# Weight pairs of the second mixture: which of them are made ready at which turn

## The chip, the cores and the metric

The kernel runs on one core of a Trainium2 chip. A time is the device time of one execution in microseconds; where several runs are given it is their median. The engines are named as in the profile: PE is TensorE (PEld its weight loads), DVE is VectorE, ACT is ScalarE, POOL is GpSimd and SP the engine whose queue issues the DMAs.

## What is computed

Three parts follow one another: an attention that keeps the 32 largest scores of a row, a mixture of 8 experts in which each of 2304 tokens goes to one expert, and a second mixture in which every token goes through every expert. Only the second mixture is changed. Cut to that:

```python
def _moe2_ref(x, w_gate, w1, w2):            # x: 2304 x 512, w1: 8 x 512 x 1024, w2: 8 x 1024 x 512
    logits = x @ w_gate
    logits = logits - logits.max()
    P = np.exp(logits)
    for _ in range(8):
        P /= P.sum(1, keepdims=True) + 1e-09
        P /= P.sum(0, keepdims=True) + 1e-09
        P *= N / E
    out = np.zeros((N, D))
    for e in range(E):
        h = np.maximum(x @ w1[e], 0.0)
        out += P[:, e:e + 1] * (h @ w2[e])
    return out
```

## The kernel before

**Split numbers.** Every matrix product is made of three passes: a float is split into a high part (`...h`, a rounded copy that ScalarE makes, line 117) and a low part (`...l`, what the copy left out, a subtraction, line 118), and `mm3` adds high x high, high x low and low x high (lines 848 to 850, in another order of operands for the second product). So weights have to be split before they are used.

**Steps.** The second mixture goes through 8 experts (`e`), for each through 9 blocks of 256 tokens (`blk`), for each through 4 quarters of the hidden layer (`i`): 288 steps, counted by `s`; 36 of them are an expert. In step s TensorE first makes the hidden quarter in one PSUM buffer `ph`, 24 matmuls (`first`, line 1089), and then takes the quarter of the step before through w2 into the banks, 21 matmuls (`second`, line 1183). There is one `ph`: the next step's matmuls may start only when ScalarE (`z`, line 1104) and VectorE (four operations on `z`, line 1103) have read it. ScalarE then makes `hh` in two parts (lines 1105 and 1111) and VectorE `hl` in two (lines 1112 and 1113), which the next step's `second` reads. The 21 matmuls stand for 24: `second` works by Strassen's scheme with seven products of quarters, so w2 needs sums of its quarters.

**Sum pieces.** After a block's fourth quarter `gather_up` (line 1125) lists the operations that turn the seven products into the output: one copy on ScalarE and, on VectorE, sums that read a bank (line 1142) and, from expert 1 on, puts into `acc` (line 1148, all operands in SBUF); 12 in all (8 or 10 in expert 0, two stores more in expert 7). `settle(k)` issues the next k of them.

**Weight pairs.** An expert's w1 and w2 are each four pairs of 128 rows of the hidden layer; pair i is used in quarter i. To make a w1 pair is one step: two ScalarE copies and two GpSimd subtractions (`w1h`, `w1l`). To make a w2 pair has two halves (`strassen`, line 125). Half a: `w2h` on ScalarE and `w2l` on VectorE, twice each (256 and 512 columns), and then four sums of the raw tiles on GpSimd (`raw`, line 129). Half b, which reads what these leave: `w2h`, `w2l`, `w3h`, `w3l`. A pair may be made when its buffer is free: 6 w1 pairs and 5 w2 pairs are kept, so that pairs 2 and 3 of the next expert's w1, and 1 to 3 of its w2, can be made only when the last block (s % 36 from 32 on) has used the present expert's. The pair that becomes free after these belongs to the expert beyond the next. A loaded pair waits in `queue`; `loads` (line 905) keeps one w1 pair and two w2 pairs in it, and the DMAs stand on SP's queue in that order.

**What sets the order.** The loop over s writes out, for each step, the operations of `first`, `second`, the sum pieces (`settle`, line 1252) and then the weight work (`work`, line 1253); each engine takes its own in this order. The work and the pieces written at the end of turn s run on ScalarE and VectorE between the `hl` of step s and the `z` of step s + 1, so in step s + 1. `work(2)` takes up to two items of the queue a turn, begun ones first, then by number, as soon as their buffers are free. In turns 1 to 18 the gate's normalisation (`sink`: `sk`, `ck`, lines 1071 to 1085) stands there too.

Of the kernel before, what the change touches and what calls it, by code (L numbers as in the profile page):

```python
# [22 lines left out]
N = B * S  # L23
# [44 lines left out]
def fused_kernel(ctx, tc, qT, kT, vv, wg1, w1a, w2a, wg2, w1b, w2b, out):  # L68
# [37 lines left out]
    def w_load(pool, src, tag, bufs):  # L106
        raw = pool.tile([128, 2, 256], F32, name="raw", tag=tag, bufs=bufs)
        nc.sync.dma_start(raw.rearrange("p a b -> p (a b)"), src)
        return raw

    def w_tiles(name, pool=None, bufs=NFC // 2):
        pool, k = pool or wpool, {"w1": 4, "w2": 5, "w3": 2}[name]
        return [pool.tile([128, k, 256], F32R, name=name + x, tag=name + x, bufs=bufs) for x in "hl"]

    def split(t, s, raw, eng):

        return [lambda: A.activation(t[0][:, s], raw, AF.Copy),  # L117
                lambda: eng.tensor_tensor(out=t[1][:, s], in0=raw, in1=t[0][:, s], op=OP.subtract)]  # L118
# [6 lines left out]
    def strassen(t, t2, b1, b2):  # L125


        b11, b12, b21, b22 = b1[:, 0], b1[:, 1], b2[:, 0], b2[:, 1]
        seq = [lambda o=o, x=x, y=y, op=op: G.tensor_tensor(out=o, in0=x, in1=y, op=op)  # L129
                for o, x, y, op in ((b11, b12, b11, OP.subtract), (b12, b22, b12, OP.subtract),  # L130
                                    (b22, b11, b22, OP.subtract), (b21, b21, b22, OP.add))]
        return [split(t, slice(0, 1), b1[:, 0:1], V) + split(t, slice(1, 3), b2, V), seq,
                split(t, slice(3, 5), b1, V) + split(t2, slice(0, 2), b2, V)]
# [698 lines left out]
    def ids_out():  # L832

        for k in range(3):
            nc.sync.dma_start(id_dram.rearrange("(e k p) o -> p k e o", k=3, p=96)[:, k], g96[:96, k, :, None])

    def ids_in():
        nc.sync.dma_start(slot_ids, id_dram.rearrange("(t p) o -> p (t o)", p=128))
# [17 lines left out]
    gone = {"w1": 0, "w2": 0}  # L856
    loaded = {"w1": NFC // 2, "w2": NFC // 2}
    queue = []
    turns = [0]

    more = {}

    def places(n, g):
        return NFC // 2 + (EXTRA[n] if g >= 36 else 0)

    def make(n, g, raws):
        at = (more[n], EXTRA[n]) if g >= 36 and (g - 36) % places(n, g) < EXTRA[n] else ()
        W[n, g] = t = w_tiles(n, *at)
        if n == "w2" and g >= 32:
            W["w3", g] = w_tiles("w3", *(at or (w3,)))  # L870
            return strassen(t, W["w3", g], *raws)
        eng = (V, G) if g < 32 else (G, G)
        return [[x for f in range(2) for x in split(t, slice(2 * f, 2 * f + 2), raws[f], eng[f])]]

    def load(n):
        g = loaded[n]
        loaded[n] += 1
        e, i = divmod(g % 32, 4)
        src = ((w1a, w1b) if n == "w1" else (w2a, w2b))[g // 32]
        raws = [w_load(rw, src[e, 2 * i + f], n, 2 if n == "w1" else 4) for f in range(2)]  # L880
        queue.append([n, g, raws, None, 0])

    def work(budget):

        turns[0] += 1
        after = []
        for item in sorted(queue, key=lambda q: (-q[4], q[1], q[0])):
            n, g, raws, stages, second_turn = item
            if g >= gone[n] + places(n, g) or budget < 1 or g >= 36 and not more:
                continue  # L890
            budget -= 1
            if stages is None:
                item[3] = stages = make(n, g, raws)
            for f in stages.pop(0):
                f()
            if stages and second_turn == 0:
                item[4] = 1
                after += stages.pop(0)
            if not stages:
                queue.remove(item)  # L900
        for f in after:
            f()
        loads()

    def loads():
        for n, room in (("w1", 1), ("w2", 2)):
            while loaded[n] < 8 * NFC and sum(q[0] == n for q in queue) < room:
                load(n)

    def need(n, g):  # L910
        for item in list(queue):
            if item[:2] == [n, g]:
                for stage in item[3] or make(n, g, item[2]):
                    for f in stage:
                        f()
                queue.remove(item)
        return W[n, g]
# [5 lines left out]
    def banks(k):  # L923
        return bank[k].rearrange("p a b -> p (a b)")

    def half_bank(k):
        return bank[k // 2][:, k % 2]
# [16 lines left out]
    def turn(xg, d, parts, pt=None, ks=(0, 1, 2)):  # L944
        if not parts:
            parts += [xg_p.tile([128, NDC, CAP], F32R, name=n, bufs=2) for n in ("xgh", "xgl")]
        if pt is None:
            pt = ps.tile([128, 2, 256], F32, name="ph").rearrange("p a b -> p (a b)")
        for k in ks:
            PE.transpose(pt[:, k * 96:(k + 1) * 96], xg[k][:96, d * 128:(d + 1) * 128], identf[:96, :96])  # L950

        def after():
            A.activation(parts[0][:, d], pt[:, :CAP], AF.Copy)
            V.tensor_tensor(out=parts[1][:, d], in0=pt[:, :CAP], in1=parts[0][:, d], op=OP.subtract)
        return after
# [24 lines left out]
    def load_x(blk):  # L980
        t = x_tiles(xs, 2)
        for k in range(2):
            nc.sync.dma_start(all_of(t[k]).bitcast(F32), xp_dram[blk][k])
        return [(t[0][:, d], t[1][:, d]) for d in range(NDC)]
# [17 lines left out]
    for k in range(3):  # L1002
        for i in range(GBUSY[k]):
            PE.matmul(banks(4), onesb, onesb[:, None, :].to_broadcast([128, 4, 128]), start=True, stop=True)
        after = [turn(xg, d, nxt, banks(d), (k,)) for d in range(NDC)]
# [3 lines left out]
    for e in range(E):  # L1009
        x, nxt = nxt, []  # L1010
        for f in range(NFC):
            w1 = need("w1", 4 * e + f // 2)
# [74 lines left out]
    sink = [(logits_end, max_a), (max_t, max_b)] + [(lambda pm: None, rows), (sums_t, columns)] * 8  # L1087
# [95 lines left out]
    def second(e, blk, i, h):  # L1183
        w2 = need("w2", 32 + 4 * e + i)
        for k in range(7):
            q = (0, 5, 1, 3, 6, 4, 2)[k]
            w = [x[:, q] for x in w2] if q < 5 else [x[:, q - 5] for x in W["w3", 32 + 4 * e + i]]
            mm3(half_bank(half(e, blk, k)), (h[0][:, k], h[1][:, k]), w,
                i == 0 and k in (0, 1, 3, 5), i == NFC // 2 - 1, skip_group_check=True)

    nb = N // 256
    pend, sums = None, []

    def settle(k):
        for _, g in sums[:k]:
            g()
        del sums[:k]

    steps = E * nb * 4
    for s in range(steps + 1):  # L1200
        eb, i = divmod(s, 4)
        e, blk = divmod(eb, nb)

        pm = half_bank(13 if (s - 1) // 4 % 2 == 0 else 5)
        if s < steps:
            if i == 0:
                x = xa.pop(0)
            h = first(need("w1", 32 + 4 * e + i), x)
            if i == 3 and eb + 2 < E * nb:
                xa.append(load_x((blk + 2) % nb))  # L1210
            if blk == nb - 1:
                gone["w1"] += 1
        if s == 40:
            ids_out()
        if s == 80:
            ids_in()
        if s and sink:
            sink[0][0](pm)
        if pend is None:
            second1(*last1)  # L1220
            part1.close()
            sx = turned.enter_context(tc.tile_pool(name="sx", bufs=1))
        else:
            while sums and sums[0][0] < pend[0] * nb + pend[1] - 1:
                settle(1)
            second(*pend)
            if pend[1] == nb - 1:
                gone["w2"] += 1
            if pend[2] == 3:
                b = pend[0] * nb + pend[1]  # L1230
                sums += [(b, g) for g in gather_up(*pend[:2])]
        if s == steps:
            settle(len(sums))
            break
        if s and sink:
            sink.pop(0)[1](pm)
            if not sink:
                sums += scales
        pend = (e, blk, i, h)
        if s < nb - halved:  # L1240

            xt = x_tiles(sx, 2)
            for d in range(NDC):
                split_x(xt, halved + s, d)
        if s == 3:
            turned.close()
            ac = late["ac"] = ctx.enter_context(tc.tile_pool(name="ac", bufs=1))
            late["acc"] = ac.tile([128, NT, D], F32, name="acc")
        if s == 6:
            more["w1"] = ctx.enter_context(tc.tile_pool(name="w1x", bufs=1))  # L1250
            more["w2"] = ctx.enter_context(tc.tile_pool(name="w2x", bufs=1))
        settle(5 if len(sums) > 12 or sink else 3)
        work(2)


# [42 lines left out]
```

## Time and profile before

| what | value |
|---|---|
| median of 3 runs | 2373.21 us (2372.59 to 2375.51) |
| the profiled execution | 2370.71 us, of which the span of its instructions 2368.9 |
| granted TensorE clock, mean over the span | 0.983 of full speed (1.00 in the second mixture) |
| the second mixture | from about 775 us to the end, 67% of the span |
| PE busy in the span | 2274.4 us (96%), 19592 matmuls |
| DVE, ACT, POOL busy | 1682.4 (71%), 1184.6 (50%), 709.9 us (30%) |

A matmul here takes 0.28 us from start to end, and the next one starts some 0.12 us after it: they overlap, so TensorE's share of busy time says little. What counts is how many matmuls run in a stretch, and where one starts late. The profile gives for each line how often an engine stood idle before it and what ended that wait; the views of single stretches show what stood in the way.

### The profile page before, as it was taken

The numbers are of one execution on the slowest core, as the hardware profiler recorded it, in microseconds if no ns is written. First come the engines' busy times: TensorE is split into PE (matmuls) and PEld (weight loads), VectorE is DVE, ScalarE is ACT, GpSimd is POOL, SyncE is SP. The second block draws the span as 40 slices with busy tenths as digits, with TensorE's granted clock in tenths as the row PEclk, the third lists the DMA queues.
The fourth block names the chain that finished last, engine by engine and source line by source line (L and its number), as shares of the span: only waits on it lengthen the run. The fifth ranks groups of instructions, "written<-read, shape, count | busy, mean of one in ns | idle before, by whom it ended". The sixth has DMA issues, their size and how long they took to land.

```text
span 2368.9 us, 49352 instructions
## 1 busy us (share of the span) xinstructions
PE 2274.4 (96%) x19592; PEld 2157.8 (91%) x19592; DVE 1682.4 (71%) x4320; ACT 1184.6 (50%) x2549; POOL 709.9 (30%) x792
## 2 busy tenths in 40 slices
PE   9999999949999899999999999999999999999998
PEld 6888888728999899999999999999999999999998
DVE  8999999873444676766776686686677668667665
ACT  8999999714555433533443343353344334334332
POOL 6888888604445200400210030040021003002011
PEclk9999999869999999999999999999999999999999
DMA  2102010015665411311221131131122113112111
GB/s 80 56 28 66 26 57 15 21 68 162 203 203 182 166 55 55 118 44 55 90 79 47 63 116 37 54 119 43 54 90 79 48 63 114 40 54 72 70 69 50
DMA packets 78048, 184.29 MB, mean 78 GB/s; under 512 B 13424, under 2 KB 13680, under 8 KB 77808
## 3 DMA queue, kind: packets, MB, share of 16 engines
q1 hardware_dynamic: 74832, 171.61, 21.8%
q0 software_dynamic: 2976, 9.44, 1.1%
q8 instruction: 156, 2.56, 0.4%
q14 instruction: 84, 0.69, 0.1%
HBM read 162.13 MB, written 18.88 MB: 76 GB/s over the span
## 4 chain that ended last, share of the span: by engine, by line
issue 41%; PE 25%; POOL 5%; DVE 3%; DMA 2%; ACT 1%; POOLq 0%; SPq 0%; DVEq 0%; ACTq 0%
PE bank L848 5%; PE bank L850 5%; PE bank L849 5%; POOL raw L129 4%; PE ph L848 3%; PE ph L849 3%; PE ph L850 3%; POOL w1l L118 1%; DMA raw<-in_w1b_dram 1%; DVE z L1103 1%; DVE w2l L118 1%; POOL out_dram L1169 0%; PE bank L961 0%; DVE hl L1113 0%; ACT w1h L117 0%
## 5 line engine op out<-in xcount | busy, mean ns | idle before, releaser
L848 PE MATMUL ph<-xh,w1h 128*128 128x256 f32 x2304 | 649.5, 282 | 40.1 <-DVE z L1103 26.6
L849 PE MATMUL ph<-xl,w1h 128*128 128x256 f32 x2304 | 646.1, 280 | 1.0 <-DMA xl<-xpl 1.0
L850 PE MATMUL ph<-xh,w1l 128*128 128x256 f32 x2304 | 645.9, 280 | 0.0
L1103 DVE SCALAR_TENSOR_TENSOR z<-ph,z 128x128 f32<-128x128 f32 x1152 | 308.2, 288 | 425.0 <-ACT z L1104 405.3
L1104 ACT ACTIVATE z<-ph 128x512 f32<-128x512 f32 x288 | 171.6, 596 | 691.3 <-PE ph L850 690.9
L118 POOL TENSOR_TENSOR w1l<-raw,w1h 128x512 fp32r<-128x512 f32 x92 | 122.6, 1345 | 1213.4 <-ACT w1h L117 1200.5
L848 PEld LDWEIGHTS ph<-xh,w1h 128*128 128x128 f32 x2304 | 434.2, 188 | 47.4 <-issue 45.4
L849 PEld LDWEIGHTS ph<-xl,w1h 128*128 128x128 f32 x2304 | 433.8, 188 | 1.3 <-DMA xl<-xpl 1.3
L850 PEld LDWEIGHTS ph<-xh,w1l 128*128 128x128 f32 x2304 | 433.8, 188 | 0.0
L848 PE MATMUL bank<-w2h,hh 128*128 128x256 f32 x1440 | 405.2, 281 | 0.0
L850 PE MATMUL bank<-w2h,hl 128*128 128x256 f32 x1440 | 404.1, 281 | 0.0
L849 PE MATMUL bank<-w2l,hh 128*128 128x256 f32 x1440 | 403.4, 280 | 0.0
L1111 ACT ACTIVATE hh<-z 128x512 fp32r<-128x512 f32 x288 | 182.2, 633 | 220.0 <-DVE z L1103 220.0
L850 PEld LDWEIGHTS bank<-w2h,hl 128*128 128x128 f32 x1440 | 271.7, 189 | 0.0
L849 PEld LDWEIGHTS bank<-w2l,hh 128*128 128x128 f32 x1440 | 271.5, 189 | 0.0
L848 PEld LDWEIGHTS bank<-w2h,hh 128*128 128x128 f32 x1440 | 271.1, 188 | 0.0
L1113 DVE TENSOR_TENSOR hl<-z,hh 128x512 fp32r<-128x512 f32 x288 | 214.9, 746 | 58.6 <-ACT hh L1111 58.6
L271 POOL TENSOR_TENSOR W<-W,sg 128x288 f32<-128x288 f32 x288 | 208.2, 733 | 69.4 <-ACT sg L266 68.9
L256 DVE MAX8 upper<-W 128x8 f32<-128x288 f32 x432 | 183.2, 448 | 5.7 <-POOL W L271 4.3
L338 PEld LDWEIGHTS pO<-vt,aT 128*128 128x128 f32 x1280 | 159.6, 193 | 28.2 <-issue 26.3
L1112 DVE TENSOR_TENSOR hl<-z,hh 128x384 fp32r<-128x384 f32 x288 | 170.9, 593 | 0.0
L295 POOL TENSOR_TENSOR dbuf<-S,upper 128x576 f32<-128x576 f32 x144 | 165.2, 1147 | 0.0
(234 smaller groups left out, 4804.5 us busy)
## 6 DMA issues: line engine op xcount, KB each, us to landing
xh<-xph SPq DMA_DIRECT2D x72, 512.0 KB, 3.3
xl<-xpl SPq DMA_DIRECT2D x72, 512.0 KB, 4.2
raw<-in_w1a_dram SPq DMA_DIRECT2D x64, 256.0 KB, 3.1
raw<-in_w2a_dram SPq DMA_DIRECT2D x64, 256.0 KB, 2.9
raw<-in_w2b_dram SPq DMA_DIRECT2D x64, 256.0 KB, 2.8
raw<-in_w1b_dram SPq DMA_DIRECT2D x64, 256.0 KB, 2.7
vt<-in_vv_dram SPq DMA_DIRECT2D x16, 325.0 KB, 3.8
kt<-in_kT_dram SPq DMA_DIRECT2D x16, 288.0 KB, 3.5
```

Source lines behind the costliest of these rows:

```text
L118: lambda: eng.tensor_tensor(out=t[1][:, s], in0=raw, in1=t[0][:, s], op=OP.subtract)]
L256: V.max(out=upper[:, ST[n]["at"], 8 * k:8 * k + 8], in_=ST[n]["W"])
L271: G.tensor_tensor(out=d["W"], in0=d["W"], in1=d["sg"], op=OP.mult)
L295: G.tensor_tensor(out=flat(d["D"])[:, :S], in0=flat(d["S"]), in1=upper[:, d["at"], 0:1].to_broadcast([128, S]), op=OP.subtract)
L848: PE.matmul(dst, a[0], b[0], start=start, stop=False, **kw)
L849: PE.matmul(dst, a[0], b[1], start=False, stop=False, **kw)
L850: PE.matmul(dst, a[1], b[0], start=False, stop=stop, **kw)
L1103: V.scalar_tensor_tensor(out, q[:, k], 0.0, y, op0=OP.max, op1=op)
L1104: A.activation(z[:, :4], q, AF.Relu)
L1111: A.activation(hh[:, 3:], z[:, 4:], AF.Copy)
L1112: V.tensor_tensor(out=hl[:, :3], in0=z[:, 1:4], in1=hh[:, :3], op=OP.subtract)
L1113: V.tensor_tensor(out=hl[:, 3:], in0=z[:, 4:], in1=hh[:, 3:], op=OP.subtract)
```

## The change

The second mixture's loop no longer calls `work(2)` but `chosen(s)` and `work2`. `due` gives a pair the turn in which it is first used. `chosen` looks at the queue in the order of these turns and takes at most one w2 half and one w1 pair a turn: a pair that is due within 12 turns, or, on every second turn of the quiet middle of an expert (s % 36 from 10 to 31), one pair that is due later. A w1 pair due in more than 2 turns stands back when a w2 pair is begun. The pieces of the sums are issued 2 a turn beside a w2 half, else 4 (5 while the normalisation lasts); before it was 3 (5 as long as more than 12 wait or the normalisation lasts). The first mixture still calls `work(1)`.

```diff
--- before.py
+++ after.py
@@ -859,6 +859,7 @@
     turns = [0]
 
     more = {}
+    nb = N // 256
 
     def places(n, g):
         return NFC // 2 + (EXTRA[n] if g >= 36 else 0)
@@ -906,6 +907,43 @@
         for n, room in (("w1", 1), ("w2", 2)):
             while loaded[n] < 8 * NFC and sum(q[0] == n for q in queue) < room:
                 load(n)
+
+    def due(n, g):
+
+        e, i = divmod(g - 32, 4)
+        return 4 * nb * e + i + (n == "w2")
+
+    def chosen(s):
+
+
+        quiet = 10 <= s % (4 * nb) < 4 * nb - 4
+        todo = {}
+        for item in sorted(queue, key=lambda q: due(*q[:2])):
+            n, g = item[:2]
+            if g >= gone[n] + places(n, g) or g >= 36 and not more:
+                continue
+            if due(n, g) - s <= 12 or quiet and s % 2 == 0 and not todo:
+                todo.setdefault(n, item)
+        if "w1" in todo and "w2" in todo and todo["w2"][4] == 0 and due(*todo["w1"][:2]) - s > 2:
+            del todo["w1"]
+        return [todo[n] for n in ("w2", "w1") if n in todo]
+
+    def work2(items):
+        after = []
+        for item in items:
+            n, g, raws, stages, begun = item
+            if stages is None:
+                item[3] = stages = make(n, g, raws)
+            for f in stages.pop(0):
+                f()
+            if stages and not begun:
+                item[4] = 1
+                after += stages.pop(0)
+            if not stages:
+                queue.remove(item)
+        for f in after:
+            f()
+        loads()
 
     def need(n, g):
         for item in list(queue):
@@ -1188,7 +1226,6 @@
             mm3(half_bank(half(e, blk, k)), (h[0][:, k], h[1][:, k]), w,
                 i == 0 and k in (0, 1, 3, 5), i == NFC // 2 - 1, skip_group_check=True)
 
-    nb = N // 256
     pend, sums = None, []
 
     def settle(k):
@@ -1249,8 +1286,9 @@
         if s == 6:
             more["w1"] = ctx.enter_context(tc.tile_pool(name="w1x", bufs=1))
             more["w2"] = ctx.enter_context(tc.tile_pool(name="w2x", bufs=1))
-        settle(5 if len(sums) > 12 or sink else 3)
-        work(2)
+        items = chosen(s)
+        settle(5 if sink else 2 if items and items[0][0] == "w2" else 4)
+        work2(items)
 
 
 # ---- launch: one core; the host lays the arrays out, nothing more ----
```

The change writes the same operations in another order. ScalarE's order at the turn from expert 1 to 2, before: the work of turn s = 69 (w2 half a and a w1 pair), one step, and the work of s = 70 (half b of that pair, half a of the next). `z<-ph` is the first operation of a step.

```order
L117 ACTIVATE w2h<-raw 128x256
L117 ACTIVATE w2h<-raw 128x512
L117 ACTIVATE w1h<-raw 128x512 x2
L1104 ACTIVATE z<-ph 128x512
L1105 ACTIVATE hh<-z 128x384
L1111 ACTIVATE hh<-z 128x512
L117 ACTIVATE w2h<-raw 128x512
L117 ACTIVATE w3h<-raw 128x512
L117 ACTIVATE w2h<-raw 128x256
```

And in the changed kernel, the same two turns (its lines 1142, 1143 and 1149 are 1104, 1105 and 1111 of before):

```order
L117 ACTIVATE w2h<-raw 128x256
L117 ACTIVATE w2h<-raw 128x512
L1142 ACTIVATE z<-ph 128x512
L1143 ACTIVATE hh<-z 128x384
L1149 ACTIVATE hh<-z 128x512
L117 ACTIVATE w2h<-raw 128x512
L117 ACTIVATE w3h<-raw 128x512
L117 ACTIVATE w1h<-raw 128x512 x2
L1142 ACTIVATE z<-ph 128x512
```

The w1 pair has moved from beside half a to beside half b, and the next pair's half a is gone from the second turn; it stands in the turn after it.

VectorE's order over the same two turns, before: the last put of a turn's three pieces, half a, the four `z` and two `hl` of step 70, three pieces, half b, and half a of the next pair.

```order
L1148 SCALAR_TENSOR_TENSOR acc<-u_27020,L_19455,acc 128x256
L118 TENSOR_TENSOR w2l<-raw,w2h 128x256
L118 TENSOR_TENSOR w2l<-raw,w2h 128x512
L1103 SCALAR_TENSOR_TENSOR z<-ph,z 128x128 x4
L1112 TENSOR_TENSOR hl<-z,hh 128x384
L1113 TENSOR_TENSOR hl<-z,hh 128x512
L1142 TENSOR_TENSOR c_27018<-c_27018,bank_19470 128x256
L1148 SCALAR_TENSOR_TENSOR acc<-c_27018,L_19455,acc 128x256
L1142 TENSOR_TENSOR u_27177<-u_27022,bank_19471 128x256
L118 TENSOR_TENSOR w2l<-raw,w2h 128x512
L118 TENSOR_TENSOR w3l<-raw,w3h 128x512
L118 TENSOR_TENSOR w2l<-raw,w2h 128x256
```

In the changed kernel (1186, 1141, 1150, 1151 and 1180 are 1148, 1103, 1112, 1113 and 1142 of before):

```order
L1186 SCALAR_TENSOR_TENSOR acc<-u_27020,L_19455,acc 128x256
L118 TENSOR_TENSOR w2l<-raw,w2h 128x256
L118 TENSOR_TENSOR w2l<-raw,w2h 128x512
L1141 SCALAR_TENSOR_TENSOR z<-ph,z 128x128 x4
L1150 TENSOR_TENSOR hl<-z,hh 128x384
L1151 TENSOR_TENSOR hl<-z,hh 128x512
L1180 TENSOR_TENSOR c_27018<-c_27018,bank_19470 128x256
L1186 SCALAR_TENSOR_TENSOR acc<-c_27018,L_19455,acc 128x256
L118 TENSOR_TENSOR w2l<-raw,w2h 128x512
L118 TENSOR_TENSOR w3l<-raw,w3h 128x512
L1141 SCALAR_TENSOR_TENSOR z<-ph,z 128x128 x4
```

The second turn has lost one piece and the two `w2l` of the next pair's half a; step 71's `z` follows `w3l` at once.

## Rows read from the trace of the kernel before

**Rows 1.** Waits of TensorE, 779 to 2350 us: total, times, longest.
```profile
PE ph L848 <- DVE z L1103: 26.6, 29, 1.5
```
**Rows 2.** Busy time by stretch: length, then PE, PEld, DVE, ACT, POOL (x instructions), clock, DMA.
```profile
1010.00:1157.00 147.00, 147.00 (x1245) 147.00 (x1245) 91.17 (x242) 50.15 (x89) 0.00 (x0) 1.00 0.15 51
...
963.00:2175.00 1212.00, 1180.93 (x9931) 1174.80 (x9931) 838.91 (x2035) 481.08 (x876) 172.88 (x160) 1.00 0.21 71
...
795.00:850.00 55.00, 53.26 (x443) 52.36 (x443) 45.74 (x124) 24.10 (x46) 13.27 (x12) 1.00 0.33 112
```
**Rows 3.** VectorE, a quiet step, in order of time: start, length, what, [idle before].
```profile
1156.18 1.14 DVE L1103 SCALAR_TENSOR_TENSOR z<-ph,z 128x128 f32<-128x128 f32 x4 [1.54 <-ACT z L1104]
...
1158.02 0.69 DVE L1113 TENSOR_TENSOR hl<-z,hh 128x512 fp32r<-128x512 f32 x1 [0.24 <-ACT hh L1111]
```
**Rows 4.** TensorE, first matmul after a quiet step and after a late one.
```profile
1157.83 0.29 PE L848 MATMUL ph<-xh,w1h 128*128 128x256 f32 x1
...
1169.67 0.36 PE L848 MATMUL ph<-xh,w1h 128*128 128x256 f32 x1 [1.02 <-DVE z L1103]
```
**Rows 5.** VectorE in the late step 70.
```profile
1164.85 0.48 DVE L1148 SCALAR_TENSOR_TENSOR acc<-u,L,acc 128x256 f32<-128x256 f32 x1
1165.25 3.22 DVE L118 TENSOR_TENSOR w2l<-raw,w2h 128x256 fp32r<-128x256 f32 x2
1168.39 1.12 DVE L1103 SCALAR_TENSOR_TENSOR z<-ph,z 128x128 f32<-128x128 f32 x4
```
**Rows 6.** GpSimd in the same step.
```profile
1164.92 1.57 POOL L118 TENSOR_TENSOR w1l<-raw,w1h 128x512 fp32r<-128x512 f32 x1 [3.52 <-ACT w1h L117]
...
1167.88 4.14 POOL L129 TENSOR_TENSOR raw<-raw 128x256 f32<-128x256 f32 x4
```
**Rows 7.** VectorE in the step after it.
```profile
1170.22 1.22 DVE L1113 TENSOR_TENSOR hl<-z,hh 128x512 fp32r<-128x512 f32 x1
1171.36 0.40 DVE L1142 TENSOR_TENSOR c<-c,bank 128x256 f32<-128x256 f32 x1
...
1173.77 1.01 DVE L118 TENSOR_TENSOR w2l<-raw,w2h 128x256 fp32r<-128x256 f32 x2
```
**Rows 8.** GpSimd: single operations of steps 71 and 73.
```profile
1169.94 0.94 POOL L129 TENSOR_TENSOR raw<-raw 128x256 f32<-128x256 f32 x1
...
1184.11 1.07 POOL L129 TENSOR_TENSOR raw<-raw 128x256 f32<-128x256 f32 x1
...
1186.44 2.62 POOL L118 TENSOR_TENSOR w1l<-raw,w1h 128x512 fp32r<-128x512 f32 x2 [1.26 <-ACT w1h L117]
```
**Rows 9.** ScalarE in step 73.
```profile
1185.21 0.63 ACT L117 ACTIVATE w3h<-raw 128x512 fp32r<-128x512 f32 x1 [1.08 <-POOL raw L129]
```
**Rows 10.** VectorE where GpSimd asks at nearly the same time, steps 8 and 74.
```profile
829.79 0.68 DVE L118 TENSOR_TENSOR w3l<-raw,w3h 128x512 fp32r<-128x512 f32 x1
...
1191.31 3.24 DVE L118 TENSOR_TENSOR w2l<-raw,w2h 128x256 fp32r<-128x256 f32 x2
```
**Rows 11.** GpSimd in these two steps.
```profile
829.86 3.02 POOL L118 TENSOR_TENSOR w1l<-raw,w1h 128x512 fp32r<-128x512 f32 x2 [1.27 <-ACT w1h L117]
...
1191.25 2.74 POOL L118 TENSOR_TENSOR w1l<-raw,w1h 128x512 fp32r<-128x512 f32 x2 [2.19 <-ACT w1h L117]
```
**Rows 12.** VectorE during the gate's normalisation, steps 5 and 7.
```profile
810.68 0.17 DVE L1082 TENSOR_SCALAR ck<-ck 128x8 f32<-128x8 f32 x1
...
813.05 0.42 DVE L1142 TENSOR_TENSOR acc<-u,bank 128x256 f32<-128x256 f32 x1
813.45 1.14 DVE L1103 SCALAR_TENSOR_TENSOR z<-ph,z 128x128 f32<-128x128 f32 x4
...
821.54 0.95 DVE L1082 TENSOR_SCALAR ck<-ck 128x8 f32<-128x8 f32 x1
...
822.76 0.98 DVE L1084 TENSOR_SCALAR ck<-ck 128x8 f32<-128x8 f32 x1
```
**Rows 13.** The page's list of DMA issues: KB each, us to landing.
```profile
raw<-in_w2b_dram SPq DMA_DIRECT2D x64, 256.0 KB, 2.8
```

## The prediction, made before the changed kernel had run

> **What bounds the kernel now.** I read the waits of TensorE first, over the second mixture alone (779 to 2350 us, two thirds of the span). It waits there for one thing in earnest, the release of `ph` by VectorE's `z` operations, 29 times, 26.6 us [rows 1]. The windows say where. A stretch in the middle of an expert runs 1245 matmuls in 147.00 us with TensorE busy throughout: 0.11807 us a matmul, 5.31 us for a step of 45 [rows 2]. The stretch that holds all seven turns from one expert to the next, 963 to 2175 us, runs 9931 matmuls in 1212 us; at the quiet rate they take 1172.6, so 39.4 us are lost (more than the waits add up to, since matmuls overlap and a late one hides part of its wait). The same sum for 795 to 850 us, where the first expert's weights and the next one's first pairs are made, gives 55 - 443 x 0.11807 = 2.7 us [rows 2]. So 42.1 us of the profiled 2368.9 are within this change's reach; nothing outside the second mixture moves.
>
> What a late step looks like: I set a clock to 0 at a step's first matmul. In a quiet step VectorE's four `z` operations run from 1156.18 to 1157.32, and the next step's first matmul starts at 1157.83 [rows 3, 4], when TensorE has just done the step before; that one began 5.31 us earlier, at 1152.52, so `z` starts at 3.66 on its clock. In a late one `z` ends at 1169.51 and the matmul follows at 1169.67, 0.16 us after it, with 1.02 us of idle time [rows 4, 5]. So `z` may slip by 0.51 - 0.16 = 0.35 us for nothing; each further microsecond is lost. `z` stands behind the turn's weight work in VectorE's order, and this is what makes it late.
>
> **Why the weight work is slow.** In the late step VectorE's two `w2l` took 3.22 us [rows 5]; the same two took 1.01 us a step later [rows 7]. Beside the slow ones GpSimd ran two `w1l`. The ends show turns taken whole: `acc` ends at 1165.33, GpSimd's `w1l`, begun at 1164.92, ends 1.16 us later at 1166.49 [rows 5, 6], and only then `w2l`. Operations that read a PSUM bank keep their time (`c`, 0.40 us, [rows 7]), those with two SBUF inputs wait (`hl` 1.22 us behind a `raw` of GpSimd that ends at 1170.88, [rows 7, 8]: it ends 0.56 us after it).
> The Trainium skill, page "SBUF — State Buffer", section "Who interferes with whom", has this as a rule: a DVE instruction with two SBUF inputs and a GpSimd instruction that reads SBUF exclude each other, and "Whoever issues first gets the shared pair for the whole instruction". The trace agrees (3.22 against 1.01 us). By this rule a collision costs all or next to nothing, by who issues first; if the two shared bandwidth instead, every overlap would cost a part, and the sum below would lie between its two ends.
>
> **The change, part by part.**
> *Order at a turn.* Before, turns s = 69 to 74 (that of expert 1 to 2; other turns alike) issue w2 a + w1, w2 b + a, b + a, b + w1, a + w1, b, where a is the first half of a w2 pair and b the second. Now 68 to 74 issue w1, a, b + w1, a, b, a, b, with two pieces of the sums instead of three beside each half. Removed from the turn: two w1 steps and one w2 pair (two halves), which go to four turns of the quiet middle.
> *A turn with one half.* After `hl` (1158.02 to 1158.71, [rows 3], so it ends at 0.88) VectorE has a sum piece from PSUM (0.42), one put (0.48, [rows 5]), and 1.01 us for half a or 2 x 0.68 for half b [rows 7, 10]: 0.88 + 0.90 + 1.36 = 3.1, less than the 3.66 at which `z` can start. GpSimd has only the four `raw`, and they start behind `w2l`. So these steps go to 5.31 us. Cover: 0.5 us of VectorE time and then the 0.35 us slack.
> *The turn with b and w1 (s = 70, running in step 71).* Here both engines meet again. Let R be the end of GpSimd's fourth `raw`. ScalarE starts `w3h` just behind it, then `w1h` twice, and GpSimd starts `w1l`: in the trace such a `raw` ends at 1185.18, `w3h` starts at 1185.21, `w1l` at 1186.44 [rows 8, 9], so `w1l` asks for the port at R + 1.26. VectorE: `hl` waits for the fourth `raw` and ends R + 0.55, then `c` and `acc` (0.40 and 0.48, each issued some 0.08 before the one ahead ends, with 0.04 between `c` and `acc`), so `w2l` is issued at R + 0.55 - 0.08 + 0.40 + 0.04 + 0.48 - 0.08 = R + 1.31. GpSimd is ahead by 0.05 us, less where ScalarE is held by the `w2h` before. In the trace GpSimd won where it started 0.06 us ahead (`w1l` 1191.25, `w2l` 1191.31: 3.24 us for two), and VectorE where it was 0.07 ahead (`w3l` 829.79, 0.68 us; `w1l` 829.86) [rows 10, 11]. I take GpSimd as first. Then from the end of `acc` (R + 1.39): `w1l` 1.16, `w2l` 0.55, `w1l` 1.16, `w3l` 0.55, so `z` starts at R + 4.7. That sums to 3.4, where the row has 3.14 with a half-sized first `w2l` [rows 5]. R: the `raw` start behind the first `w2l`, 2.1 into step 70; in the late step they took 4.14 us [rows 6], with both parts of `hl` in their way, and one of them 0.94 for it [rows 8]; here one part is, so 3.8 by my count. That makes R 0.6 to 0.9 into step 71. `z` starts at 5.3 to 5.6 in place of 3.66; less 0.35, 1.25 to 1.6 us. I take 1.25, the lower R, for that one `hl`. Lower end 0.1 (VectorE first). The turn of expert 0 to 1 has a scale and a PSUM piece there, so `w2l` is issued near R + 1.1, ahead of `w1l`: nothing. Six turns: 6 x 1.25 = 7.5 us, bounds 0.6 and 9.6.
> *Quiet middle.* A w1 turn there stands beside four sum pieces, two of them puts. `w1l` delays each put by up to one GpSimd operation: `hl` 0.88, piece 1.2, put behind the first `w1l` (0.8 to 2.1) 2.35, piece 2.7, put behind the second (to 3.5) 3.8: `z` slips by about 0.05, inside the slack. Zero, upper bound 0.5 us in each of 12 such turns, 6 us. The w2 halves there take two pieces, like the turns above: zero.
> *Sum pieces by fours* (4, 4, 4, none): four pieces are 1.8 to 1.9 us on VectorE behind 0.88: done by 2.8, hidden before 3.66. Their banks are freed a step earlier or as late as before.
> *First expert.* The start (s = 0 to 3) now has one w2 half a turn and w1 once: I put its share of the 2.7 us at zero left. But pairs of expert 1 now fall on turns s = 10 to 16, in which the gate normalisation and up to five pieces stand on VectorE. At s = 12, in a step like the one where the last piece runs until 813.47, just when `z` starts [rows 12], half a adds 1.01, less 0.35: 0.65 lost. At s = 16, beside the same pieces, `w1l` holds up two small `ck` operations (0.95 and 0.98 us where one alone takes 0.17, [rows 12]): 1.6, less 0.35, 1.25. Together 1.9, bounds 0.5 and 3.
> *Loads.* As many DMAs as before, on SP's queue in the order in which pairs are finished; a w2 load lands 2.8 us after issue [rows 13] and has at least two steps. Zero.
> Sum: 42.1 - 7.5 - 1.9 = 32.7 us less. The profiled execution took 2370.7 in all (1.8 around its span): 2338.0. The median of the runs, 2373.2, lies 2.5 above it: 2340.
>
> **Rivals.**
> 1. *VectorE is first in step 71.* The margin is 0.05 us, and a `raw` that ends before 0.5 leaves `w3h` bound by ScalarE and moves `w1l` behind `w2l`. Against it: both chains hang on R. The step then loses 0.1: 2340 - 6 x 1.15 = 2333.
> 2. *The quiet turns pay as well.* VectorE's margin at a quiet w1 turn is 0.3 us by my count. If a put lands behind one more GpSimd operation (1.16), 12 turns cost about 1 each: 2352; if the 12 w2 halves did too, 2364, near no change. For it: where two met, a `w1l` grew to 1.57 us [rows 6]. Against it: no SBUF-only operation but the puts stands there.
> 3. *A pair comes too late (slower).* Pair 3 of w2 is now finished in step 75, some 3 us in, and first read 2.8 us into step 76: 5.1 us spare. If its load or its halves slip, TensorE waits for weights once a turn. It eats the gain (42/7 = 6 us a turn) once the slip passes 11 us, two turns; at 13 us the kernel takes 2340 + 7 x 8 = 2396. Against it: the load has two steps and needs 2.8 us.
> That pairs would not be moved at all is excluded by the order of the instructions shown with the change.
>
> **Numbers.** Forecast 0.58, rival 1 0.25, rival 2 0.13, rival 3 0.04. The range 2330 to 2352 holds the first two with an error of 3 us of the medians, the bounds of step 71, of the first expert, and half of rival 2. No change means within 0.2%, 4.7 us, which is about what can be told. Faster 0.93 (all of the first two and most of rival 2), same 0.04, slower 0.03.
>
> **What would show it.** Right: between the turns and in them steps of 5.3 us, but one near 6.5 in each of six turns, with `w2l` and `w3l` over 3 us together beside two `w1l`; TensorE's waits for `z` down to some 8 in number; the two late steps at s = 13 and 17. Rival 1: no such step, `w1l` above 1.5 us instead. Rival 2: late steps twice or four times between turns. Wrong altogether: TensorE waiting for `w2h`, `w3l` or a DMA.

## The result, and the profile after

The changed kernel took 2339.82 us (median of 4 runs, 2339.17 to 2340.85) beside 2372.9 us of the kernel before (4 runs on the same chip, 2371.94 to 2375.51): 0.9857 of it, 95% interval 0.9845 to 0.987. The forecast was 2340.

TensorE's waits in the second mixture (779 to 2350 us; total, times, longest) answer to [rows 1]:

```profile
PE ph L848 <- issue: 6.5, 6, 1.1
PE ph L848 <- DVE z L1141: 1.8, 3, 1.2
PE ph L849 <- DMA xl<-xpl: 0.6, 1, 0.6
```

Six are put down to "issue", time for which the profile shows no releaser; the rows of step 71 below show that such a matmul follows the end of `z`. The kernel before has such waits too, beside the 29 of [rows 1], and the prediction left them out:

```profile
PE ph L848 <- issue: 6.3, 10, 1.1
```

So 39 waits of 32.9 us have become 9 of 8.3 us. The wait for `xl`, a DMA of the tokens, is in step 0; in the trace of before it stands there too (1.0 us, ahead of this window). The same stretches of the expert's quiet middle, of the turns, and of the first expert as in [rows 2], moved by a few us so that they begin and end between turns, and the 55 us behind the last one:

```profile
1010.00:1155.00 145.00, 145.00 (x1229) 145.00 (x1228) 94.72 (x244) 53.99 (x98) 8.67 (x8) 1.00 0.19 63
960.00:2150.00 1190.00, 1183.47 (x10011) 1182.41 (x10010) 825.50 (x2044) 484.56 (x882) 163.82 (x160) 1.00 0.22 72
...
795.00:850.00 55.00, 54.92 (x467) 54.71 (x466) 44.19 (x122) 21.80 (x40) 9.43 (x8) 1.00 0.29 99
...
850.00:905.00 55.00, 53.50 (x450) 52.95 (x449) 43.55 (x122) 21.29 (x39) 6.39 (x6) 1.00 0.20 67
```

In the quiet middle GpSimd now works (8.67 us where it stood still), and TensorE still takes 145 / 1229 = 0.11798 us a matmul: the pairs put there cost nothing. At this rate the 10011 matmuls of the turns need 1181.1 of 1190 us: 8.9 are lost, where it was 39.4 (one matmul more or less in the quiet count moves this by 1). The first expert's loss has moved from the third stretch to the fourth, 55 - 450 x 0.11798 = 1.9 us by this rough count (an edge can fall one matmul either way, 0.12 us).

The six late steps that are left are steps 71, 107, 143, 179, 215 and 251, each with b and w1 in it. Step 71 begins at 1165.13; VectorE in it (start, length, what, [idle before]) answers to [rows 5]:

```profile
1165.32 0.94 DVE L1151 TENSOR_TENSOR hl<-z,hh 128x512 fp32r<-128x512 f32 x1 [0.21 <-ACT hh L1149]
1166.18 0.41 DVE L1180 TENSOR_TENSOR c<-c,bank 128x256 f32<-128x256 f32 x1
1166.62 0.48 DVE L1186 SCALAR_TENSOR_TENSOR acc<-c,L,acc 128x256 f32<-128x256 f32 x1
1167.03 1.79 DVE L118 TENSOR_TENSOR w2l<-raw,w2h 128x512 fp32r<-128x512 f32 x1
1168.74 1.77 DVE L118 TENSOR_TENSOR w3l<-raw,w3h 128x512 fp32r<-128x512 f32 x1
1170.44 1.12 DVE L1141 SCALAR_TENSOR_TENSOR z<-ph,z 128x128 f32<-128x128 f32 x4
```

GpSimd beside it ([rows 6]):

```profile
1161.94 3.77 POOL L129 TENSOR_TENSOR raw<-raw 128x256 f32<-128x256 f32 x4 [3.89 <-DVE w2l L118]
1166.98 2.99 POOL L118 TENSOR_TENSOR w1l<-raw,w1h 128x512 fp32r<-128x512 f32 x2 [1.27 <-ACT w1h L117]
```

ScalarE beside it ([rows 9]):

```profile
1165.74 0.63 ACT L117 ACTIVATE w3h<-raw 128x512 fp32r<-128x512 f32 x1
1166.28 1.14 ACT L117 ACTIVATE w1h<-raw 128x512 fp32r<-128x512 f32 x2
```

and TensorE's first matmul after it ([rows 4]):

```profile
1171.67 0.36 PE L848 MATMUL ph<-xh,w1h 128*128 128x256 f32 x1 [1.07 <-issue]
```

`w1l` starts at 1166.98 and `w2l` at 1167.03: GpSimd is 0.05 us ahead, and `w2l` and `w3l` take 3.5 us for what elsewhere takes 1.3. `z` ends at 1171.56 and the matmul follows 0.11 us later; the step lasts 6.54 us in place of 5.30.

The seventh double turn, from expert 0 to 1 (step 35, from 973.54), shows the other order in the same trace. VectorE is 0.06 us ahead:

```profile
975.30 0.68 DVE L118 TENSOR_TENSOR w2l<-raw,w2h 128x512 fp32r<-128x512 f32 x1
975.90 1.79 DVE L118 TENSOR_TENSOR w3l<-raw,w3h 128x512 fp32r<-128x512 f32 x1
```

GpSimd beside it:

```profile
975.36 3.50 POOL L118 TENSOR_TENSOR w1l<-raw,w1h 128x512 fp32r<-128x512 f32 x2 [1.26 <-ACT w1h L117]
```

Only `w3l` waits, for one `w1l`, and the step lasts 5.30 us.

### The profile page after: what moved, and what is told of

It reads as the page before. It is cut to its first block, busy times and chain, and to the rows that moved or that the text cites. A ratio compares the mean times of both kernels' runs of the same rounds, so it can differ in the third digit from the quotient of the medians.

```text
span 2339.1 us, 49316 instructions
## 1 busy us (share of the span) xinstructions
PE 2267.6 (97%) x19592; PEld 2156.4 (92%) x19592; DVE 1667.0 (71%) x4320; ACT 1184.5 (51%) x2549; POOL 701.2 (30%) x792
## 4 chain that ended last, share of the span: by engine, by line
PE 69%; issue 5%; DVE 1%; POOL 1%; DMA 1%; ACT 0%; SPq 0%; POOLq 0%; DVEq 0%; ACTq 0%
PE bank L848 12%; PE bank L850 12%; PE bank L849 12%; PE ph L848 11%; PE ph L849 11%; PE ph L850 11%; PE bank L999 1%; POOL out_dram L1207 0%; DVE z L1141 0%; DMA xg<-x_dram,g 0%; POOL raw L129 0%; DMA xl<-xpl 0%; PE ph L988 0%; DMA raw<-in_w1b_dram 0%; DVE hl L1151 0%
## 5 line engine op out<-in xcount | busy, mean ns | idle before, releaser
L1151 DVE TENSOR_TENSOR hl<-z,hh 128x512 fp32r<-128x512 f32 x288 | 206.6, 717 | 61.8 <-ACT hh L1149 61.8
L129 POOL TENSOR_TENSOR raw<-raw 128x256 f32<-128x256 f32 x128 | 111.9, 874 | 192.4 <-DVE w2l L118 182.3
L1150 DVE TENSOR_TENSOR hl<-z,hh 128x384 fp32r<-128x384 f32 x288 | 165.7, 575 | 0.0
```

Source lines behind the costliest of these rows:

```text
L1150: V.tensor_tensor(out=hl[:, :3], in0=z[:, 1:4], in1=hh[:, :3], op=OP.subtract)
L1151: V.tensor_tensor(out=hl[:, 3:], in0=z[:, 4:], in1=hh[:, 3:], op=OP.subtract)
```

## The experiments

*Theory A:* what is left at a turn is the meeting of `w1l` and VectorE's two operations, and who asks first decides it. *Theory B:* it is load; VectorE or ScalarE has more to do in that turn than a step holds, and adding work makes it worse, taking work off better. *Theory C:* the piece counts carry a part of the gain by themselves, by keeping other steps in time. The experiments are versions of the changed kernel. Kernels 1 to 4, 5 to 8 and 9 to 12 each ran beside the kernel before on one chip, whose median there was 2373.51, 2374.25 and 2373.15 us. Beside the result it was 2372.9, so medians of different jobs can differ by 1.4 us without any edit; the lengths of single steps repeat to 0.1 us from step 3 on, in each of the four kernels that were traced twice, and are the firmer evidence.

**1. Work added on ScalarE in the double turn** (the first `w1h` copy made twice, so that GpSimd starts later):

```diff
+            if n == "w1" and len(items) == 2:
+                stages[0][0]()
             for f in stages.pop(0):
```

> Adds work: where a w2 half and a w1 pair stand in one turn, ScalarE makes the first w1h copy twice (0.62 us more, 7 or 8 times in all). Theory A (GpSimd and VectorE take the SBUF port in the order in which they ask; in the late step GpSimd's w1l asks 0.05 us before VectorE's w2l): w1l now asks 0.5 us later, VectorE's w2l goes first, w3l waits for one w1l only, z starts near 4.2 on the step's clock instead of 5.3, so the six late steps shrink from 6.55 to about 5.5 us: 6 x 1.06 = 6.4 us less, 2333.4. Rival B (the step is late because too much work stands on ScalarE and VectorE in it): no gain, up to 0.6 us more in each of seven turns: 2340 to 2344.

Measured 2331.96 us (2331.46 to 2335.4), 0.9828 (0.9815 to 0.9841). VectorE in step 71, which begins at 1164.07:

```profile
1165.98 0.69 DVE L118 TENSOR_TENSOR w2l<-raw,w2h 128x512 fp32r<-128x512 f32 x1
1166.58 0.69 DVE L118 TENSOR_TENSOR w3l<-raw,w3h 128x512 fp32r<-128x512 f32 x1
1167.72 1.15 DVE L1143 SCALAR_TENSOR_TENSOR z<-ph,z 128x128 f32<-128x128 f32 x4 [0.46 <-ACT z L1144]
```

GpSimd in it:

```profile
1166.59 3.09 POOL L118 TENSOR_TENSOR w1l<-raw,w1h 128x512 fp32r<-128x512 f32 x2 [1.93 <-ACT w1h L117]
```

One more copy of 0.6 us on ScalarE made the kernel 7.9 us faster than the changed kernel: the six steps that were late are 5.30 to 5.33 long. VectorE now takes both operations at full speed, the second one 0.01 us ahead of `w1l`, in each of the six. Theory B, as far as it is load on ScalarE, falls. The Trainium skill, page "SBUF — State Buffer", section "Who interferes with whom", says that the order of issue decides which engine blocks; this trace agrees down to a margin of 0.01 us, the finest that it shows.

**2. The `w1l` of every fourth pair on VectorE**, so that GpSimd is out of the double turn:

```diff
-        eng = (V, G) if g < 32 else (G, G)
+        eng = (V, G) if g < 32 else (V, V) if g >= 36 and g % 4 == 3 else (G, G)
```

> Moves the two w1l of the pair that shares a turn with w2's half b (pair 3 of each expert from 1 on) from GpSimd to VectorE, the engine on which the late step waits: 1.38 us more on it, no GpSimd operation to wait for. Theory A (port order): z starts near 4.5 instead of 5.3 in six turns, so these steps go from 6.55 to about 5.8, and the turn of expert 0 to 1, which was not late, loses 0.2: 4.5 us less, 2335.3. Rival B (too much work on VectorE): seven turns each up to 1.38 longer: 2346 to 2349.

Measured 2335.59 us (2333.81 to 2337.43), 0.9841 (0.9829 to 0.9854). The late steps shrank from 1.23 to 1.29 us of excess to 0.23 to 0.29, where A had left them 0.5. With the meeting gone VectorE carries 1.29 us more and is late only by what its own work then exceeds the step. That is load, and small; that more work on VectorE makes the step shorter ends Theory B. The six steps give back 6.0 us, not 4.5, and from step 1 to the last one the trace is 5.9 us shorter; that the median came out at A's 2335.3 is chance in part.

**3. One weight item a turn from s = 20 on, with the pieces of before:**

```diff
-        items = chosen(s)
-        settle(5 if sink else 2 if items and items[0][0] == "w2" else 4)
-        work2(items)
+        if s < 20:
+            ...
+        else:
+            settle(5 if len(sums) > 12 or sink else 3)
+            work(1)
```

> From turn 20 on the old rule again (no due times, no quiet middle, sum pieces by three as before), but one item of the queue a turn instead of two; turns 0 to 19 as in the changed kernel. Theory A: a w1 pair never stands beside a w2 half, so no collision is left and the six late steps go: 6 x 1.25 = 7.5 us less, 2332.3; the due times and the quiet middle are not needed for the gain. Rival C (the gain comes from making pairs of the expert beyond the next in the quiet middle and from two pieces beside a half): the turn of 11 items and three pieces costs again at least 1 us in several steps: 2345 or more.

Measured 2337.15 us (2336.82 to 2340.07), 0.9848 (0.9836 to 0.9861), 5 us over what A expected. No step of 71's kind is late, but another is. TensorE's waits:

```profile
PE bank L849 <- DVE w3l L118: 3.1, 6, 0.5
PE ph L848 <- DVE z L1141: 1.5, 2, 1.2
```

VectorE in step 76 (from 1192.85):

```profile
1195.47 0.69 DVE L118 TENSOR_TENSOR w2l<-raw,w2h 128x512 fp32r<-128x512 f32 x1
1196.07 0.69 DVE L118 TENSOR_TENSOR w3l<-raw,w3h 128x512 fp32r<-128x512 f32 x1
```

TensorE there:

```profile
1196.03 0.28 PE L848 MATMUL bank<-w3h,hh 128*128 128x256 f32 x1
1196.81 0.39 PE L849 MATMUL bank<-w3l,hh 128*128 128x256 f32 x1 [0.50 <-DVE w3l L118]
```

With one item a turn the second half of w2 pair 3 falls in the very step whose `second` reads it: `w3l` ends at 1196.76, the matmul follows at 1196.81. Six such steps are 0.78 to 0.84 longer, 4.8 us. This is rival 3 of the prediction at a smaller price. In step 76 of the changed kernel it isn't there, because the double turn brings that half a turn earlier; the double turn buys the due time and pays with the meeting. The experiment shows more. From turn 20 on this kernel differs from the one before only in taking one item a turn (`work(1)`) in place of two, with no due times and no quiet middle, and it is as fast as the changed kernel (2.7 us under it by the medians, with intervals that overlap). So one item a turn by itself gives a gain of this size. (Step 1 also took 9.61 in place of 8.07 us; see 9 to 12.)

**4. No limit on how early a pair may be made, from s = 20 on:**

```diff
-            if due(n, g) - s <= 12 or quiet and s % 2 == 0 and not todo:
+            if s >= 20 or due(n, g) - s <= 12 or quiet and s % 2 == 0 and not todo:
```

> From turn 20 on nothing is kept for the quiet middle: a pair is made as soon as its buffer is free, still at most one w2 half and one w1 pair a turn. The two w1 pairs of the expert beyond the next then stand beside halves b of the turn. Theory A: each of these turns collides like the one at s = 70, so two more late steps of about 1.25 us in each of six to seven turns: 2352 to 2357. Rival B (work in sum): the same operations spread over the same number of turns with one w2 half each, little change: 2339 to 2344.

Measured 2386.56 us (2383.1 to 2388.64), 1.0052 (1.0039 to 1.0064): slower than the kernel before, and some 30 us over what was expected. TensorE's waits:

```profile
PE bank L848 <- DVE u L1180: 20.4, 5, 4.1
PE ph L848 <- issue: 14.5, 7, 8.0
PE ph L848 <- DVE z L1141: 9.0, 7, 1.6
```

The first of the five, in step 77:

```profile
1211.51 0.58 PE L848 MATMUL bank<-w3h,hh 128*128 128x256 f32 x1 [4.08 <-DVE u L1180]
```

VectorE's sum that it waits for:

```profile
1211.04 0.41 DVE L1180 TENSOR_TENSOR u<-u,bank 128x256 f32<-128x256 f32 x1
```

And the busy time by stretch around it (columns as in [rows 2]):

```profile
1202.00:1209.50 7.50, 5.43 (x47) 5.23 (x45) 6.63 (x15) 4.42 (x9) 2.81 (x4) 1.00 0.62 214
1209.50:1216.30 6.80, 4.79 (x22) 4.79 (x23) 3.51 (x8) 0.33 (x2) 0.00 (x0) 0.50 0.06 24
```

The collisions that A expected came (1.25 us in step 71, 1.7 in 73), but the price is another. Seven half turns with two pieces each settle too few: before a block's products may overwrite a bank, what is left of the older sums is written out at once, and stands in VectorE's order behind `z` and `hl`; TensorE waits 4.08 us for a bank, and from 1209.5 us, inside this wait, to 1216.3 its granted clock is 0.50. Five turns take 6.1 us more each from this. The limit on how early a pair may be made therefore does a job that I had not named. In the changed kernel the halves of the fourth pair come in steps 85 and 87, behind turns of four pieces; here they follow the other six at once (steps 76 and 77). Which part of the limit is needed, the 12 turns or every second turn, no run shows.

**5. No pieces in the double turn**, three beside a half a:

```diff
-        settle(5 if sink else 2 if items and items[0][0] == "w2" else 4)
+        w2_half = items and items[0][0] == "w2"
+        settle(5 if sink else 4 if not w2_half else 0 if len(items) == 2 else 2 if items[0][4] else 3)
```

> Same order of weight work; only the sum pieces beside it change (from the end of the normalisation on): none in the turn in which half b and a w1 pair meet, three beside a half a, two beside a half b, else four. VectorE then comes to w2l and w3l about 0.9 us earlier in the turn at s = 70, ahead of w1l (w2l near 1.05, w3l near 1.65, w1l asks at 1.85 on the step's clock). Theory A (order of asking at the port): the six late steps go wholly, 7.5 us less: 2332.3. Rival B (sum of VectorE's work): the late step gets 0.9 us less work of the 1.25 it is late, six times: 2334.4, with steps of 5.6 left at the turns.

Measured 2331.86 us (2331.41 to 2334.38), 0.9826 (0.9813 to 0.9839). VectorE in step 71, which begins at 1163.96:

```profile
1165.36 0.68 DVE L118 TENSOR_TENSOR w2l<-raw,w2h 128x512 fp32r<-128x512 f32 x1
1165.96 0.68 DVE L118 TENSOR_TENSOR w3l<-raw,w3h 128x512 fp32r<-128x512 f32 x1
```

GpSimd in it:

```profile
1166.16 2.89 POOL L118 TENSOR_TENSOR w1l<-raw,w1h 128x512 fp32r<-128x512 f32 x2 [1.27 <-ACT w1h L117]
```

VectorE is now 0.8 us ahead and the six late steps are gone, as A expected. Both engines moved: without the two pieces `w2l` starts 1.40 us into the step (1.90 in the changed kernel), and the third piece beside half a makes the `raw` later, so that `w1l` starts at 2.20 (1.85). The same gain as in 1, where GpSimd alone was made later.

**6. The quiet middle of the first expert only from s = 20**, behind the normalisation:

```diff
-        quiet = 10 <= s % (4 * nb) < 4 * nb - 4
+        quiet = (10 if s >= 4 * nb else 20) <= s % (4 * nb) < 4 * nb - 4
```

> In the first expert alone the quiet middle begins at turn 20 instead of 10, after the gate normalisation; all else as in the changed kernel. If steps 13, 14 and 17 are late (0.44, 0.37 and 1.35 us in the trace) because weight work meets the normalisation's operations on VectorE, they go: 2.2 us less, 2337.7. Rival D (they are late because of the five sum pieces and the normalisation alone): no change, 2339.8.

Measured 2341.63 us (2341.12 to 2342.99), 0.9864 (0.9849 to 0.9879). Steps 13, 14 and 17 are on time, as expected, 2.2 us; but in the profiled run step 1 took 10.47 us instead of 8.07 and step 2 0.68 more, at half the clock, which eats it. Taken up again below.

**7. Edits 5 and 6 together.**

> The edits of the two runs before together. Theory A: no collision at the turns and none in the normalisation: 7.5 + 2.2 us less than the changed kernel, 2330.1, the fastest of all. Rival B: 2332 or more.

Measured 2331.69 us (2330.27 to 2332.5), 0.982 (0.9806 to 0.9833). From step 2 on only step 4 (0.37) is late, and step 2 by 0.1; against 1 and 5 the difference of the medians is within the error, so the medians don't decide between A and B. The steps speak for A: from step 1 to the last one the trace is 2.1 us shorter than that of 5, and step 1 began 1.8 us later.

**8. Three pieces a turn, as before the change:**

```diff
-        settle(5 if sink else 2 if items and items[0][0] == "w2" else 4)
+        settle(5 if len(sums) > 12 or sink else 3)
```

> The changed kernel's choice of weight work, but sum pieces by the old rule (3 a turn, 5 as long as more than 12 wait or the normalisation lasts). A half alone has room for three pieces: 0.88 + 1.4 + 1.36 us end at 3.6, before z at 3.66. Theory A: only the turn at s = 70 gets later, by one more piece on VectorE ahead of z (0.4 us, six times): 2342. Rival C (two pieces beside a half are needed for the gain): every one of the six turns with a half grows by 0.2 to 0.4 us, 7 times: 2348 or more.

Measured 2348.47 us (2345.98 to 2349.89), 0.9888 (0.9873 to 0.9903). The late steps are 1.69 to 1.77 over, 0.45 each more than in the changed kernel, the size that A expected; and the turn from expert 0 to 1, which was on time, collides too (step 35, 1.59). But the piece that costs is not the one ahead of `w2l` in the double turn. GpSimd around step 71, which begins at 1171.37:

```profile
1168.64 3.76 POOL L129 TENSOR_TENSOR raw<-raw 128x256 f32<-128x256 f32 x4 [4.37 <-DVE w2l L118]
1173.67 2.99 POOL L118 TENSOR_TENSOR w1l<-raw,w1h 128x512 fp32r<-128x512 f32 x2 [1.27 <-ACT w1h L117]
```

The third piece of the turn before, ahead of half a, makes the `raw` end 1.03 us into step 71 (0.58 in the changed kernel) and `w1l` start at 2.30 (1.85); GpSimd is first by 0.4 us, and the whole chain stands 0.45 us later. No step outside the double turns became late, so C falls: the pieces count only in the double turn and the turn before it. The 4.3 us of these steps leave 4 more, and these stand ahead of step 2.

**9 to 12. The changed kernel, 6, 7 and 8 once more, unaltered, side by side on another chip.** What was open: whether the half clock in step 1 belongs to a kernel (K) or to an execution or chip (X).

> The changed kernel unaltered, beside the next three on one chip. In its first trace step 1 of the second mixture took 8.07 us at the full clock. Theory K (the stretches at the half clock in the routing stage and in step 1 belong to the kernel): step 1 at 8.1 us again, about 2340. Theory X (they belong to the single execution or the chip): step 1 may take 8 to 10.5 us, and the order of the four kernels changes with it.

> The version with the quiet part of the first expert from s = 20, unaltered; first measured at 2341.6 with 10.47 us for step 1 (6.8 us of it at half clock). Theory K: the same stretch again, about 2341.5, no faster than the changed kernel. Theory X: without that stretch the 2.1 us of the first expert come through: 2337.7, or 2 us under the changed kernel's time in this job.

> No pieces in the double turn and the quiet part of the first expert from s = 20, unaltered; first measured at 2331.7 with 8.07 us for step 1. Theory K: 2331.7, step 1 at full clock. Theory X: 2330 to 2334, by the clock that it is granted.

> Three pieces a turn, unaltered; first measured at 2348.5, where the seven late steps account for 7 x 1.7 = 11.9 in place of the 7.6 of the changed kernel (4.3 us more) and the rest stood ahead of step 2. Theory K: about 2348.5, with step 1 at 9.6 us. Theory X: 2344, 4.3 us over the changed kernel in this job.

Measured, in this order: 2340.61 (2339.41 to 2341.28), 2338.35 (2338.01 to 2340.88), 2330.99 (2328.99 to 2338.39) and 2344.75 us (2340.66 to 2350.02). The stretch 785 to 800 us in the first trace of 6, then in the second (the clock is the third number from the end):

```profile
785.00:800.00 15.00, 14.80 (x101) 14.66 (x100) 11.46 (x25) 8.98 (x22) 7.31 (x6) 0.77 0.48 175
```

```profile
785.00:800.00 15.00, 14.64 (x123) 14.44 (x122) 12.89 (x29) 10.79 (x25) 7.00 (x6) 0.98 0.38 144
```

The same kernel runs 101 matmuls there in one execution and 123 in the other. Step 1 took 7.97 us in the new traces of 6 and 8, and 9.51 in that of 7, which had been clean: X holds; whether it is the execution or the chip, these runs don't tell. With it the sums close: 6 is 2.3 us under the changed kernel (2 expected), 8 is 4.1 over it (4.3 expected), and 7 is 9.6 under it, the fastest version that was run, 0.9822 of the kernel before (0.9808 to 0.9835). With 2 to 9 us between the runs of one kernel such a close fit of medians is in part chance; the step lengths of these traces agree with the first ones to 0.1 us from step 3 on.

## Why the prediction was right, step by step

- *What is in reach.* Right. The turns lost 39.4 us before and 8.9 after. In the profiled executions the time fell by 2370.71 - 2340.85 = 29.9 us, 2.8 less than the 32.7 worked out; the second mixture's first steps began 2.0 us later in that of after (step 1 at 785.83, before 783.82), in a part where both kernels are the same. From there to the end it is 31.8. That the median met the forecast to 0.2 us is chance in part: the profiled execution lay 2.5 us below the median before, and 1.0 above it after. One thing the working did not separate: not all that the turns lost was a meeting with `w1l`. In the turn of expert 1 to 2 of before, steps 70 and 74 (half a beside `w1l`) lost 2.9 us and step 73 (half b and `w1l`) 0.6, but steps 71 and 72 lost 2.6 us with no `w1l` in them: there VectorE had three pieces, half b and the next half a, with `hl` slowed by the `raw`. The change took both causes away at once, and no run parts them; who asks first is shown to decide only for the six steps that were left.
- *Turns with one half.* Right: they take 5.30 to 5.36 us, up to 5.40 behind a late step; the turns of before, with two items, had steps up to 1.76 over.
- *The turn with b and w1.* Right in place, order and size. R was 0.58 us into step 71 (0.6 to 0.9 taken, the lower end chosen); `w1l` came at R + 1.27 and `w2l` at R + 1.32, 0.05 us apart as worked out from [rows 5, 7 to 9]; the six steps lost 1.23 to 1.29 us where 1.25 was taken, and the turn of expert 0 to 1 nothing. This was also the step with the most luck in it: a margin of 0.05 us, summed from rows read to 0.01, decided over 7.6 us. Experiments 1 and 5 are rival 1 made true: 2332.0 and 2331.9, where 2333 was worked out for it. The 1 us between them is the 0.1 a step that was left to it (0.0 was measured) and the 0.08 to 0.10 us that the step behind a late one loses, which the sum left out.
- *Quiet middle and sum pieces by fours.* Right at zero, and rival 2 falls: 0.11798 us a matmul with GpSimd at work. The mechanism is right too. In step 83 (from 1230.26), with `w1l` from 1230.98 to 1233.73, both puts wait and `z` still starts at 3.67:

```profile
1231.47 1.09 DVE L1186 SCALAR_TENSOR_TENSOR acc<-u,L,acc 128x256 f32<-128x256 f32 x1
1232.93 1.08 DVE L1186 SCALAR_TENSOR_TENSOR acc<-u,L,acc 128x256 f32<-128x256 f32 x1
1233.93 1.13 DVE L1141 SCALAR_TENSOR_TENSOR z<-ph,z 128x128 f32<-128x128 f32 x4
```

  For the banks the working looked at the turns with four pieces only; experiment 4 shows that a row of turns with two leaves the banks taken, and that the kernel is then slower than before.
- *First expert.* Right in place, and short: 1.9 us worked out, 2.5 measured. Step 13 lost 0.44 (0.65 worked out) and step 17 1.35 (1.25). VectorE in step 17, beside `w1l` from 877.18 to 879.72:

```profile
877.28 1.21 DVE L1120 TENSOR_SCALAR ck<-ck 128x8 f32<-128x8 f32 x1
878.53 0.20 DVE L1121 RECIPROCAL ck<-ck 128x8 f32<-128x8 f32 x1
878.77 0.98 DVE L1122 TENSOR_SCALAR ck<-ck 128x8 f32<-128x8 f32 x1
```

  The two small scalings wait for one GpSimd operation each, as in [rows 12]; the reciprocal between them does not. What the sum lacked are steps 4 and 14, 0.34 and 0.37. In both `raw` holds up `hl` (in step 14 both parts, 0.85 and 1.22 us), so what follows on VectorE ends later. In step 14 these are the row sums of the normalisation, and TensorE's own matmul for the column sums, which stands ahead of `second`, waits for them:

```profile
862.40 0.28 PE L850 MATMUL ph<-xh,w1l 128*128 128x256 f32 x1
862.71 0.51 PE L1115 MATMUL bank<-L,onesf 128*128 128x144 f32 x2
```

  In step 4 the column sums are on time (807.46), but half b stands in the step whose `second` reads it, and TensorE waits for `w3l`, which ends at 808.36. VectorE, then TensorE, whose matmul would have come at 808.18:

```profile
807.67 0.69 DVE L118 TENSOR_TENSOR w3l<-raw,w3h 128x512 fp32r<-128x512 f32 x1
```

```profile
808.06 0.28 PE L848 MATMUL bank<-w3h,hh 128*128 128x256 f32 x1
808.42 0.39 PE L849 MATMUL bank<-w3l,hh 128*128 128x256 f32 x1
```

  The start (s = 0 to 3) had been put at zero left; step 4 is the turn s = 3, and before it lost 0.07 us. I had followed VectorE to `z` and not the other readers of its work.
- *Loads, and rival 3.* Right for the loads and the turns: no wait for a weight's DMA stands in the trace of after, and none for a weight at a turn. But the sign named for "wrong altogether", TensorE waiting for `w3l`, is there once, in step 4, for 0.24 us; the list of waits does not show it, since the matmuls ahead of it were still running. Experiment 3 shows how near it was: one turn later for the same half costs 0.8 us a turn.
- *The chances.* Rival 1 had 0.25 and was 0.05 us away; all six turns repeat one pattern to 0.05 us, so it could only come out six times or not at all, and 0.25 was, if anything, low for a margin no wider than the sum's own error.

## What to carry to other kernels

Where two engines exclude each other for whole operations, don't count load alone: write down when each asks, to 0.05 us, and if they come near one another, move one of them clear; a later start of the engine that nobody waits for can be enough (1), and added work that delays it can make a kernel faster. When work is spread over quiet turns, list what those turns did before (here the sum pieces that free the banks, and the pair that just came in time): in experiments 3 and 4 the new bottleneck was what the other order had done by the way. And follow a late operation to all of its readers (step 4), not only to the one that was late before. And before a few microseconds are explained by an edit, compare the granted clock of the stretches that the edit doesn't touch.

## What the runs showed of the hardware beyond this

- Whoever was first by as little as 0.01 us kept its time, in all six turns of the trace of experiment 1; the other's two operations took 3.09 us there (`w1l`, step 71), where the two took 2.54 in step 17 of the changed kernel.
- A scaling of 128 x 8 numbers, 0.17 us alone, is held for a whole GpSimd operation (1.21 us); a reciprocal of the same size is not (0.20).
- TensorE's clock fell to 0.50 (1.2 GHz) for 6.8 us in and behind a 4.08 us wait between stretches at 1.00 (experiment 4); the step took 6.1 us more in all.
- Executions of one kernel differ by 2 to 9 us (2328.99 to 2338.39 for 7). The two traced ones of 7 took 2331.89 and 2338.39 us, and all of the 6.5 us stands ahead of step 2 (begun at 794.60 and 801.10). There the granted clock differs: from 512 to 552 us its mean was 0.75 and 0.63, from 785 to 800 us, around step 1, 1.00 and 0.73. What sets this is open; no run here varied it.
